# Handing the last three token tiles to the first expert by one-hot products, with its first weights split during the attention

## The chip, the cores and the metric

The kernel runs on one core of a Trainium2 chip (trn2). The metric is the device time of one execution in microseconds (us), as the median of several runs. One execution is also recorded by the hardware profiler; its rows are the trace. In the rows, PE is TensorE (matmuls), PEld its weight loads, DVE is VectorE, ACT is ScalarE, POOL is GpSimd and SP is SyncE, which issues most of the DMA transfers; PEclk is the clock granted to TensorE as a share of 2.4 GHz, so that 0.50 is 1.2 GHz. Times in the trace count from the start of the recorded span.

## What is computed

Three stages follow one another. The attention takes 2 batches of 8 heads, 768 tokens of 64 numbers each, and masks every pair of tokens whose clusters differ. Its result is read as 1536 tokens of 512 numbers. A mixture of 8 experts then sends each token through the one expert that it picks (512 to 1024, ReLU, and back to 512). A bilinear layer ends the kernel. Everything is float32.

```python
scores = scale * np.matmul(q, k.transpose(0, 1, 3, 2))
scores = np.where(mask, scores, -1000000000.0)
attn = np.exp(scores - max); attn = attn / (sum + 1e-09)
x = (attn @ v).transpose(0, 2, 1, 3).reshape(B * S, H * D)
# experts
expert_idx = np.argmax(xn @ en.T / tau, axis=1)
for e in range(E):
    mask = expert_idx == e
    h = np.maximum(x[mask] @ w1[e], 0.0)
    out[mask] = gate_w[mask, None] * (h @ w2[e])
# bilinear
return (out @ w_a) * (out @ w_b) @ w_out
```

## The kernel before

**Order.** The kernel is written under a manual schedule: each engine runs its instructions in the order in which the Python code issues them, and an engine stands at an instruction until the semaphores that it waits for have come. The issue order is the only plan there is.

**Attention.** There are 96 steps, twelve for each of eight pairs (batch, two heads). Step s issues: the exponentials E(s+1) (ACT, L478), the six transposes et(s) (PE, L493) and their two copies to SBUF, ET (half on ACT at L497, half on DVE at L499), the scores sc(s+2) (PE, L464 and L465), their row maximum nmx(s+2) (DVE, L473), and then pieces of older work from Python generators: the products pv with the values (PE, L520), their copy xt (ACT, L526), the product px that turns the result back into token rows and gives the expert logits (PE, L534), and the scaled rows xrow and xlog (DVE, L536). Steps 84 to 95 are the last pair. Token rows come in tiles of 128; a batch has six, 0 to 5, and those of the second batch are finished in groups: tiles 0 to 2, then 3 and 4, then 5. So et_90 below means the transposes of step 90, and px_7_5 the product px of pair 7 for tile 5.

**Picking and routing.** For each group, `pick_gen` finds every token's expert (the one-hot array oh_all), and `route_gen` counts, with small matmuls pos on PE, which slot of its expert the token gets; slot_i holds the slots. An expert has CAP = 256 slots. POOL then writes the rows of each tile to their slots in the DRAM tensor xs_d, one indirect DMA for a tile (the scatter, L584). After the last group, cnt_p (L717) counts the tokens of each expert, and `most` (L721) is the fullest expert's count. Every engine loads `most` into a register (L906) and branches on it (L907): code for experts with over 256 tokens is skipped here.

**Experts.** The weights of an expert come as chunks of 512x512, in parts of 128x512, which SP loads into `raw` (L129). Each part is split into a high part w hi (ACT cast, L818) and a low part w lo (DVE subtraction, L824), and a product is the sum of three matmuls (high by high, high by low, low by high). Before the branch ACT casts the eight parts of the first two chunks, `split_hi(8)`; after the branch DVE subtracts them, `split_lo()`. Beside that SP loads the 256 rows of expert 0 from xs_d (`load_xe(0)`, behind all scatters), PE keeps busy with 14 matmuls on dummy data (`keep_warm`, wps) and transposes the rows (`trans_x`, xT, L888), and ACT and DVE split them (xTh, L890, and xTl, L892). The main loop then counts G from 0 to 63 for eight experts of eight blocks: `layer1(G)` issues h (twelve matmuls, L900), ACT's ReLU hh (L967) and DVE's rest hl (L968); `layer2(G-2)` issues y (six matmuls, L983).

**Gates.** In the later experts the generator `gates()` advances once for each G. After some arithmetic it issues, for each of the twelve token tiles, one POOL scatter of 8-byte rows into the DRAM table tab_d (L782), each followed by a POOL memset of one element of `tick` (L787).

Of the kernel before, what the change touches and what calls it, by code (L numbers as in the profile page):

```python
# [22 lines left out]
P = 128  # L23
FAR = float(2.0 ** 100)
CAP = 256
# [10 lines left out]
FL3 = 14  # L36
# [6 lines left out]
def kernel(  # L43
# [39 lines left out]
    psa = att_stack.enter_context(tc.tile_pool(name="psa", bufs=1, space=PSUM))  # L83
# [33 lines left out]
    def load_raw():  # L117
# [12 lines left out]
        for j in range(cnt):  # L130
            raw[m + j] = t[:, j]

# [371 lines left out]
    def pv_gen(g, between=None):  # L504
# [10 lines left out]
        per, every = ((3 if t0 else 2), 1) if pp == NP - 1 else (2, 2)  # L515
# [17 lines left out]
        for t in range(n):  # L533
            nc.tensor.matmul(px[:, t, :], xt[:, t * P:(t + 1) * P], rmat[:, hp, :], start=True, stop=True)  # L534
        for c0, w, dst in ((2 * D, NE, lg[:, tsl, 2 * hp * NE:2 * (hp + 1) * NE]), (0, D, xs[:, tsl, 2 * hp * D:2 * (hp + 1) * D])):
# [30 lines left out]
    def route_gen(b, t0, n):  # L566
# [7 lines left out]
        for j in range(n - 1):  # L574
            nc.tensor.matmul(pp_[:, j + 1:, :], ones, oh[:, j:j + 1, :].to_broadcast([P, n - 1 - j, NE]), start=False, stop=(j == n - 2))
        sl = rt.tile([P, HALF, NE], F32, tag="r_sl", name=f"sl_{b}_{t0}", bufs=2)[:, :n]
        nc.vector.tensor_tensor(out=sl, in0=pp_, in1=oh, op=ALU.mult)
        with nc.allow_low_precision(reason="one whole number below 2^24 and zeros"):
            nc.vector.tensor_reduce(out=slot_i[:, gsl], in_=sl, axis=AX.X, op=ALU.add)
# [10 lines left out]
        for j in range(n):  # L590
            yield
            junk = rt.tile([P, DM], F32, tag="r_junk", name=f"junk_{b}_{t0}_{j}")
            nc.scalar.activation(junk, x_rows[b][:, t0 + j, :], AF.Square, accum_out=n2_all[:, gsl.start + j:gsl.start + j + 1])
# [57 lines left out]
    for s in range(nst):  # L651
# [14 lines left out]
        if s in (4 * SPP + 1, 4 * SPP + 3, 4 * SPP + 7, 4 * SPP + 9):  # L666
            load_raw()
        if s + 1 < nst:
            expo(s + 1)
        etrans(s)  # L670
        if 2 <= s < SPP:
            next(rest, None)
# [19 lines left out]
        if s + 1 == nst or steps[s + 1][0] != g_:  # L692
            def then(g=g_):
# [4 lines left out]
                elif s + 1 < nst:  # L698
# [4 lines left out]
                    yield from route_gen(b, t0, n)  # L703
                else:
                    yield from pv_gen(g, pick_gen(b, t0, n))
# [5 lines left out]
    work = later + work  # L711
    while work:
        work = [g for g in work if next(g, 0) != 0]


    cnt_p = psa.tile([P, NE], F32, tag="rot", name="cnt_p", bufs=3)
    nc.tensor.matmul(cnt_p, ones, cum.rearrange("p o e -> p (o e)"), start=True, stop=True)  # L717
    cnt = left.tile([P, NE, 1], F32, name="cnt")
# [47 lines left out]
    def gates():  # L766
# [14 lines left out]
        for g in range(B * NT):  # L781
# [5 lines left out]
            nc.gpsimd.memset(tick[:, g:g + 1], 0.0)  # L787
# [7 lines left out]
    ps_s = ctx.enter_context(tc.tile_pool(name="ps_s", bufs=2 * CT, space=PSUM))  # L795
    ps_t = ctx.enter_context(tc.tile_pool(name="ps_t", bufs=1, space=PSUM))
    big = ctx.enter_context(tc.tile_pool(name="big", bufs=1))

# [4 lines left out]

    def open_part():
        n, j = divmod(nsplit[0], 4)
        if j == 0:
            hl[n] = big.tile([P, 2, 4, 512], F32R, tag=f"w{n % NSLOT}", name=f"w_{n}")
        w = raw.pop(nsplit[0])
        nsplit[0] += 1
        return w, hl[n][:, 0, j, :], hl[n][:, 1, j, :]  # L810

    halves = []

    def split_hi(m):
        for _ in range(m):
            load_raw()
            w, hi, lo = open_part()
            nc.scalar.copy(hi, w)  # L818
            halves.append((w, hi, lo))

    def split_lo():
        while halves:
            w, hi, lo = halves.pop(0)
            nc.vector.tensor_sub(lo, w, hi)  # L824
            ndone[0] += 1
            load_raw()

    def split_some(m):
# [321 lines left out]
```

## Time and profile before

| what | value |
|---|---|
| time of the kernel before, median of 3 runs | 821.48 us (821.29 to 823.35) |
| time of the profiled execution | 823.11 us |
| span of its trace | 821.4 us |
| PE busy | 787.9 us, 96% of the span |
| DVE busy | 487.4 us, 59% |
| ACT busy | 397.9 us, 48% |
| POOL busy | 90.8 us, 11% |

PE is busy nearly all the time, so what can be won lies where it is not. The page cuts the span into 40 slices; PE falls below nine tenths in the first slice and in slices 15 and 16 (the way from the attention to the experts, about 288 to 308 us), and in slice 22 (435 to 442 us, amid the experts), and its clock falls with it. How to read a row of a timeline: start, length, engine, line, operation, what it writes <- what it reads, shape, count, and in brackets how long the engine stood idle before it and whose end let it go.

### The profile page before, as it was taken

To read this page: it belongs to the slowest core of one execution; us is meant where nothing else is said; L and a number is where in the kernel's file an instruction comes from. 1 tells how busy PE (TensorE), PEld (TensorE's weight loads), DVE (VectorE), ACT (ScalarE), POOL (GpSimd) and SP (SyncE) were. 2 spreads that over 40 slices of the span, in tenths; PEclk is the share of its full clock that TensorE was granted. 3 is DMA by queue.
4 is the path that set the end of the run, shared out by engine and by line. 5 is a ranking of instruction groups with operands and counts; after the bars stand their busy time and mean duration, and the time that the engine had idled before them with its cause. 6 is when DMAs were issued, how large, how long until landed. Compare 5 with 4: busy or idle time off the path is not lost.

```text
span 821.4 us, 13806 instructions
## 1 busy us (share of the span) xinstructions
PE 787.9 (96%) x5359; PEld 675.5 (82%) x5359; DVE 487.4 (59%) x996; ACT 397.9 (48%) x859; POOL 90.8 (11%) x122
## 2 busy tenths in 40 slices
PE   8899999999999949999997999999999999999997
PEld 5667777776777629999996999999999999999996
DVE  7777577775767557886674699999432222222221
ACT  4666766766666546765553555555221221211211
POOL 5212203233000030000023000000010010010101
PEclk9999999999999979999998999999999999999999
DMA  6137313353120038987768766764010000000000
GB/s 194 41 100 251 85 31 97 74 169 93 30 59 10 1 121 306 322 283 232 226 189 176 220 215 188 241 201 139 1 53 27 26 26 1 1 26 1 28 1 26
DMA packets 45388, 92.62 MB, mean 113 GB/s; under 512 B 6265, under 2 KB 15097, under 8 KB 45313
## 3 DMA queue, kind: packets, MB, share of 16 engines
q1 hardware_dynamic: 41104, 81.67, 33.5%
q0 software_dynamic: 2304, 6.31, 2.0%
q10 hardware_dynamic: 1904, 3.67, 1.3%
q8 instruction: 44, 0.72, 0.4%
q14 instruction: 32, 0.25, 0.1%
HBM read 69.27 MB, written 14.69 MB: 102 GB/s over the span
## 4 chain that ended last, share of the span: by engine, by line
PE 33%; issue 26%; another core or an unknown queue 1%; POOL 1%; DVE 1%; ACT 0%; POOLq 0%; DVEq 0%; ACTq 0%
PE h L900 11%; PE y L983 10%; PE ab L900 8%; PE o L1053 3%; POOL out_dram L1064 1%; PE xT L888 1%; DVE w L824 1%; ACT w L818 0%; POOLq L1145 0%; POOL tick L1069 0%; ACT hh L967 0%; DVE ot L1063 0%; DVE xTh L890 0%; PE xT_('b', 0)_0_6645 L888 0%
## 5 line engine op out<-in xcount | busy, mean ns | idle before, releaser
L1026 DVE TENSOR_TENSOR ga<-ab,ga 128x256 f32<-128x256 f32 x72 | 30.5, 423 | 153.5 <-ACT ga L1025 153.5
L478 ACT ACTIVATE E<-sc,nmx 128x768 f32<-128x768 f32 x96 | 86.7, 903 | 58.7 <-DVE nmx L473 46.1
L1025 ACT COPY ga<-ab 128x256 f32<-128x256 f32 x72 | 26.8, 372 | 164.6 <-PE ab L900 164.6
L473 DVE TENSOR_REDUCE nmx<-sc 128x1 f32<-128x768 f32 x96 | 91.4, 953 | 16.8 <-PE sc L465 15.1
L493 PEld LDWEIGHTS et<-ident,E 128*128 128x128 f32 x576 | 62.5, 141 | 36.1 <-ACT ET L497 12.6
L1053 PE MATMUL o<-w,gh 128*128 128x512 f32 x288 | 90.7, 396 | 0.0
L824 DVE TENSOR_TENSOR w<-raw,w 128x512 fp32r<-128x512 f32 x128 | 82.5, 687 | 13.4 <-ACT w L818 12.0
L493 PE MATMUL et<-ident,E 128*128 128x128 f32 x576 | 82.3, 279 | 5.8 <-ACT E L478 4.3
L499 DVE COPY ET<-et 128x384 f32<-128x384 f32 x96 | 52.7, 549 | 55.0 <-PE et L493 52.2
L983 PE MATMUL y<-w,hh 128*128 128x512 f32 x256 | 81.6, 400 | 0.5 <-issue 0.5
L900 PEld LDWEIGHTS h<-xTh,w 128*128 128x128 f32 x512 | 71.2, 194 | 13.2 <-DVE hl L968 4.8
L818 ACT CAST w<-raw 128x512 fp32r<-128x512 f32 x128 | 72.9, 619 | 18.4 <-DMA raw<-in_moe_w_dram 12.1
L900 PE MATMUL h<-xTh,w 128*128 128x256 f32 x512 | 73.5, 287 | 7.4 <-DVE hl L968 4.4
L520 PE MATMUL pv<-ET,v 128*64 128x384 f32 (+2 forms) x408 | 73.2, 479 | 0.8 <-ACT ET L497 0.6
L464 PE MATMUL sc<-K,Q 80*128 80x512 f32 x192 | 72.7, 379 | 0.0
L465 PE MATMUL sc<-K,Q 128*128 128x512 f32 x192 | 61.3, 340 | 0.0
L967 ACT ACTIVATE hh<-h 128x256 fp32r<-128x256 f32 x64 | 24.5, 383 | 66.8 <-PE h L900 56.6
L1053 PE MATMUL o<-w,gl 128*128 128x512 f32 x144 | 56.1, 389 | 0.0
L1029 ACT CAST gh<-ga 128x256 fp32r<-128x256 f32 x72 | 29.3, 407 | 53.6 <-DVE ga L1026 53.6
L1053 PEld LDWEIGHTS o<-w,gh 128*128 128x128 f32 x288 | 49.6, 190 | 6.5
L1064 POOL DMA_INDIRECT out_dram<-ot,res x12 | 11.5, 958 | 364.9 <-DVE ot L1063 363.6
L983 PE MATMUL y<-w,hl 128*128 128x512 f32 x128 | 50.0, 391 | 0.0
(266 smaller groups left out, 1498.3 us busy)
## 6 DMA issues: line engine op xcount, KB each, us to landing
raw<-in_moe_w_dram SPq DMA_DIRECT2D x64, 512.0 KB
raw<-in_moe_w_a_dram SPq DMA_DIRECT2D x12, 512.0 KB
raw<-in_moe_w_b_dram SPq DMA_DIRECT2D x12, 512.0 KB
raw<-in_moe_w_out_dram SPq DMA_DIRECT2D x12, 512.0 KB
xs_d<-zero SPq DMA_DIRECT2D x8, 512.0 KB
ys_d<-ys SPq DMA_DIRECT2D x8, 512.0 KB
xe<-xs_d ACTq DMA_DIRECT2D x7, 512.0 KB
v<-in_v_dram SPq DMA_DIRECT2D x8, 384.0 KB
```

The lines of the kernel that those rows point to most:

```text
L464: nc.tensor.matmul(ps[:, lo:hi], Q3[:, qs], K3[:, h * S + lo:h * S + hi], start=True, stop=False)
L465: nc.tensor.matmul(ps[:, lo:hi], Q2[:, qs], K2[:, h * S + lo:h * S + hi], start=False, stop=True)
L473: nc.vector.tensor_reduce(out=nmx[pp][:, h, t:t + 1], in_=sc[s], axis=AX.X, op=ALU.max, negate=True)
L478: nc.scalar.activation(e, sc.pop(s), AF.Exp, bias=nmx[pp][:, h, t:t + 1], accum_out=sums[pp][:, t, h:h + 1])
L493: nc.tensor.transpose(pt[:, j * P:(j + 1) * P], e[:, kt * P:(kt + 1) * P], ident)
L499: nc.vector.tensor_copy(dst, src)
L520: nc.tensor.matmul(pv[h * D:(h + 1) * D, :], vt[:, h, kt, :], ets[g, h][:, kt, :n * P], start=(kt == 0), stop=(kt == NT - 1))
L818: nc.scalar.copy(hi, w)
L824: nc.vector.tensor_sub(lo, w, hi)
L900: nc.tensor.matmul(ps, s_, m_, start=(i == 0), stop=(i == len(ops) - 1))
L983: nc.tensor.matmul(ys_ps[e][t], s_[:, t * P:(t + 1) * P], w[:, m_, ff, :], start=(f == 0 and i == 0), stop=(f == NF - 1 and i == 2))
L1053: nc.tensor.matmul(o_ps[ck][t], s_[:, t * P:(t + 1) * P], w_[:, m_], start=(f == 0 and i == 0), stop=(f == NF2 - 1 and j == len(o_f[ck]) - ...
```

## The change

There are five edits, all in one kernel file.

1. **One-hot products.** The rows of the last three token tiles of the second batch (3, 4 and 5) no longer reach expert 0 through DRAM. Once the nine other tiles are scattered, SP loads expert 0's rows (`near_load`). PE transposes them with eight plain matmuls against the identity into two PSUM tiles (`near_trans`), and for each of the three tiles eight more matmuls (`inject`) add the tile's rows, as high and low parts, times a one-hot matrix of slots. The scatters of these three tiles still go out, for the experts behind. The one-hot matrices come from ACT (Abs, then Relu) for tiles 3 and 4 and from DVE for tile 5. The high and low parts of the rows are made during the attention for the columns of the first six heads (a cast of 128x1152 on ACT, a subtraction on POOL), and at the end for the rest.
2. **The end of the attention.** The product pv_7_0 runs in two pieces of six instead of three of four, tiles 0 to 2 are picked and routed some steps earlier, the squares of the rows (junk) are reordered, and the last work list is walked in reverse.
3. **First weights.** The four parts of the first chunk, w_0, are split in steps 85 to 88 (`split_some(1)`), the next two before the branch (`split_hi(2)`). `keep_warm(14)`, `load_xe(0)` and `trans_x` of expert 0 are gone; `load_xe(1)` is issued in block G = 1.
4. **Branch.** The condition has a label and a hint for PE that the branch is likely taken, and the new pools wait for single tiles instead of for the whole pool before them.
5. **Gates.** The memset of `tick` after each scatter into tab_d becomes a copy of one element of the newest hh.

```diff
-    def pv_gen(g, between=None):
+    def pv_gen(g, between=None, behind_px=None):
-        per, every = ((3 if t0 else 2), 1) if pp == NP - 1 else (2, 2)
+        per, every = (3, 1) if pp == NP - 1 else (2, 2)
...
+        if near and t0 > HALF:
+            inject(1)
...
+                nc.scalar.activation(far, near_t["iota"], AF.Abs, bias=ns[:, j:j + 1])
+                nc.scalar.activation(near_t["oneh"][:, j, :], far, AF.Relu, scale=-1.0, bias=1.0)
...
+    def near_hi(t0, n, c0, c1):
+        nc.scalar.copy(near_t["hi"][:, t0:t0 + n, c0:c1], x_rows[B - 1][:, HALF + t0:HALF + t0 + n, c0:c1])
+    def near_load():
+        i = nc.sync.dma_start(out=near_t["xe"], in_=xs_d[:CAP, :].rearrange("(c p) d -> p c d", p=P))
+    def near_trans():
+        near_t["ps"] = [psa.tile([P, 2, CAP], F32, tag="sc", name=f"xT_near_{u}", bufs=2) for u in range(2)]
+        for j in range(DC):
+            for t in range(CT):
+                nc.tensor.matmul(near_t["ps"][j // 2][:, j % 2, t * P:(t + 1) * P], near_t["xe"][:, t, j * P:(j + 1) * P], ident,
+                                 start=(j % 2 == 0 and t == 0), stop=False)
+    def inject(t):
+        for j in range(DC):
+            for k_ in ("hi", "lo"):
+                nc.tensor.matmul(near_t["ps"][j // 2][:, j % 2, :], near_t[k_][:, t, j * P:(j + 1) * P], near_t["oneh"][:, t, :],
+                                 start=False, stop=(t == HALF - 1 and j % 2 == 1 and k_ == "lo"))
...
+        if s == (NP - 1) * SPP + SPP // 2 + 1:
+            near_hi(0, HALF, 0, 2 * (HP - 1) * D)
+            near_lo(nc.gpsimd, 0, HALF, 0, 2 * (HP - 1) * D)
+        if s == (NP - 1) * SPP + 10:
+            near_load()
         if s + 1 < nst:
             expo(s + 1)
         etrans(s)
+        if pp == NP - 1 and i in (1, 2, 3, 4):
+            split_some(1)
...
+    tc.mark_branch_hint_location("rare", "LikelyTaken", engines=[mybir.EngineType.PE])
...
-            nc.gpsimd.memset(tick[:, g:g + 1], 0.0)
+            nc.gpsimd.tensor_copy(tick[:, g:g + 1], hh()[0:1, 0:1])
...
-    load_xe(0)
-    split_hi(8)
+    split_hi(2)
     n_most = nc.values_load(most, min_val=0, max_val=NTOK)
-    with tc.If(n_most > CAP):
+    with tc.If(n_most > CAP, label="rare"):
...
-    keep_warm(ps_s.tile([P, DM], F32, tag="sc", name="wps2"), FL3)
     split_lo()
-    trans_x(0, xe_t[0], True)
-    load_xe(1)
...
+            if G == 1:
+                load_xe(1)
```

The first place is DVE in steps 85 and 86. A row gives the line, the operation, what it writes <- what it reads, and the semaphores waited for. Before:

```order
L473 TENSOR_REDUCE nmx_2979<-sc_3028 128x1 [waits PE_49]
L499 COPY ET_0_0_3017<-et_1_3045 128x3x128 [waits PE_49]
L473 TENSOR_REDUCE nmx_2979<-sc_3050 128x1 [waits PE_49]
L499 COPY ET_0_0_3017<-et_1_3063 128x3x128 [waits PE_49]
L473 TENSOR_REDUCE nmx_2979<-sc_3068 128x1 [waits PE_49]
```

and in the changed kernel:

```order
L505 TENSOR_REDUCE nmx_2980<-sc_3035 128x1 [waits PE_49]
L531 COPY ET_0_0_3024<-et_1_3052 128x3x128 [waits PE_49]
L156 TENSOR_TENSOR w_3057<-raw_1929,w_3057 128x512 [waits DMAHW2_49,Activation_49]
L505 TENSOR_REDUCE nmx_2980<-sc_3060 128x1 [waits PE_49]
L531 COPY ET_0_0_3024<-et_1_3073 128x3x128 [waits PE_49]
L156 TENSOR_TENSOR w_3057<-raw_1929,w_3057 128x512 [waits Activation_49]
L505 TENSOR_REDUCE nmx_2980<-sc_3082 128x1 [waits PE_49]
```

The subtraction w lo (L156) now stands between ET(s) and nmx(s+2), and it waits for ACT. On ACT the same steps of the changed kernel read:

```order
L510 ACTIVATE E_3045,sums_2979<-sc_3035,nmx_2980 128x768 [waits DVE_49,Activation_49]
L529 COPY ET_0_0_3024<-et_0_3047 128x3x128 [waits PE_49]
L150 CAST w_3057<-raw_1929 128x512
L510 ACTIVATE E_3066,sums_2979<-sc_3060,nmx_2980 128x768 [waits DVE_49,Activation_49]
L529 COPY ET_0_0_3024<-et_0_3068 128x3x128 [waits PE_49]
```

The cast w hi (L150) stands behind E(s+1) and ET(s) and ahead of E(s+2); before, E(s+2) followed ET(s) at once.

The second place is PE between the last px and the branch. Before, pos of tile 5 followed pos of tiles 3 and 4, and cnt_p and the load of `most` came right behind:

```order
L534 MATMUL px_5_3346<-rmat,xt_5_3342 128x144 [waits DVE_49,Activation_49]
...
L572 MATMUL pos_3_3351<-cum,ones 128x16 [waits PE_49]
...
L572 MATMUL pos_5_3374<-cum,ones 128x8 [waits PE_49]
L573 LDWEIGHTS tri
L573 MATMUL pos_5_3374<-oh_all,tri 128x8 [waits DVE_49]
L717 LDWEIGHTS ones [waits DVE_49]
L717 MATMUL cnt_p<-cum,ones 128x8 [waits PE_49]
L906 TENSOR_LOAD most [waits DVE_49]
L907 COMPARE_AND_BRANCH
```

In the changed kernel:

```order
L566 MATMUL px_5_3396<-rmat,xt_5_3374 128x144 [waits Activation_49]
L681 MATMUL xT_near_3398<-ident,xe_near 128x128 [waits DMAHW3_49]
L681 MATMUL xT_near_3398<-ident,xe_near 128x128 x3
L681 MATMUL xT_near_3399<-ident,xe_near 128x128 x4
L687 MATMUL xT_near_3398<-oneh,x_near_hi 128x256 [waits Activation_49]
L687 MATMUL xT_near_3398<-oneh,x_near_lo 128x256 [waits Pool_49]
...
L606 MATMUL pos_5_3426<-cum,ones 128x8 [waits PE_49]
L607 LDWEIGHTS tri
L607 MATMUL pos_5_3426<-oh_all,tri 128x8 [waits DVE_49]
L687 MATMUL xT_near_3398<-oneh,x_near_hi 128x256 [waits Activation_49]
```

Eight transposes, which wait for the load of xe_near, and the eight products of tile 3 now stand ahead of pos of tile 5; the products of tiles 4 and 5 follow around cnt_p.

The third place is POOL in the gates. Before:

```order
L782 DMA tab_d<-id_gate,slot_i 1536x2 [waits DMASW4_49,DVE_49,Pool_49]
L787 MEMSET tick 1x1
L782 DMA tab_d<-id_gate,slot_i 1536x2 [waits DMASW5_49]
L787 MEMSET tick 1x1
L782 DMA tab_d<-id_gate,slot_i 1536x2 [waits DMASW6_49]
```

In the changed kernel:

```order
L907 DMA tab_d<-id_gate,slot_i 1536x2 [waits DMASW4_49,DVE_49,Pool_49]
L913 CAST tick<-hh_5917 1x1 [waits Activation_49]
L907 DMA tab_d<-id_gate,slot_i 1536x2 [waits DMASW5_49]
L913 CAST tick<-hh_5948 1x1 [waits Activation_49]
L907 DMA tab_d<-id_gate,slot_i 1536x2 [waits DMASW6_49]
```

Between two scatters POOL now waits for the ReLU of one more block.

## Rows read from the trace of the kernel before

**Rows 1.** Windows: length, busy us of PE, PEld, DVE, ACT, POOL, clock, DMA, GB/s.
```profile
256.00:268.00 12.00, 12.00 (x80) 8.27 (x78) 8.11 (x13) 7.53 (x17) 0.00 (x0) 1.00 0.01 1
291.00:298.00 7.00, 0.48 (x4) 0.20 (x5) 2.72 (x19) 1.52 (x5) 4.42 (x11) 0.50 0.51 192
308.00:313.00 5.00, 5.00 (x29) 4.88 (x29) 1.99 (x4) 1.81 (x4) 0.00 (x0) 0.66 1.02 381
```
**Rows 2.** The page's groups of w lo and w hi: busy, mean ns, idle before.
```profile
L824 DVE TENSOR_TENSOR w<-raw,w 128x512 fp32r<-128x512 f32 x128 | 82.5, 687 | 13.4 <-ACT w L818 12.0
L818 ACT CAST w<-raw 128x512 fp32r<-128x512 f32 x128 | 72.9, 619 | 18.4 <-DMA raw<-in_moe_w_dram 12.1
```
**Rows 3.** Timeline of ACT in steps 85 to 89: start, length, operation.
```profile
258.48 0.90 ACT L478 ACTIVATE E<-sc,nmx 128x768 f32<-128x768 f32 x1 [0.24 <-DVE nmx L473]
...
259.37 0.47 ACT L497 COPY ET<-et 128x384 f32<-128x384 f32 x1
...
267.65 0.91 ACT L478 ACTIVATE E<-sc,nmx 128x768 f32<-128x768 f32 x1
```
**Rows 4.** Timeline of DVE in the same steps.
```profile
260.15 0.96 DVE L473 TENSOR_REDUCE nmx<-sc 128x1 f32<-128x768 f32 x1 [0.16 <-PE sc L465]
...
268.97 0.55 DVE L536 TENSOR_TENSOR xrow<-px,rs 128x384 f32<-128x384 f32 x1
```
**Rows 5.** Timeline of PE: the transposes of steps 90 and 95.
```profile
271.11 0.88 PE L493 MATMUL et<-ident,E 128*128 128x128 f32 x6
...
285.58 0.87 PE L493 MATMUL et<-ident,E 128*128 128x128 f32 x6
```
**Rows 6.** Timeline of PE from the last px to the first y.
```profile
289.00 0.51 PE L534 MATMUL px<-rmat,xt 128*128 128x144 f32 x2 [0.36 <-ACT xt L526]
...
302.57 1.04 PE L888 MATMUL xT<-ident,xe 128*128 128x128 f32 x8
304.06 0.74 PE L900 MATMUL h<-xTh,w 128*128 128x256 f32 x4 [0.46 <-ACT xTh L890]
307.35 0.74 PE L900 MATMUL h<-xTh,w 128*128 128x256 f32 x4 [2.55 <-DVE xTh L890]
...
313.02 0.63 PE L983 MATMUL y<-w,hh 128*128 128x512 f32 x2
```
**Rows 7.** Timeline of SP: the load of expert 0's rows.
```profile
298.78 0.37 SPq L875 DMA_DIRECT2D xe<-xs_d  x1
```
**Rows 8.** Timeline of POOL behind the last scatter.
```profile
295.96 0.20 POOL L728 MEMSET scan<- 128x24 f32 x2
```
**Rows 9.** Timeline of DVE: the end of the scan.
```profile
297.55 0.15 DVE L739 CAST ov_i<-cnt 1x8 int32<-1x8 f32 x1
```
**Rows 10.** The branch's line: sequencer, count, duration ns, first and last start.
```profile
L907 DVEq EVENT_SEMAPHORE  x2: 21/21/21, 300.9 to 301.0; - x2
...
L907 PEldq COMPARE_BRANCH  x1: 4112/4112/4112, 293.6 to 293.6; - x1
```
**Rows 11.** Windows amid the experts, same columns.
```profile
428.00:436.00 8.00, 8.00 (x54) 7.32 (x53) 4.05 (x7) 3.11 (x7) 6.68 (x13) 1.00 0.82 146
436.00:442.00 6.00, 1.61 (x7) 0.83 (x5) 0.01 (x1) 0.42 (x2) 3.23 (x8) 0.93 1.02 144
442.00:448.00 6.00, 5.53 (x23) 5.33 (x24) 4.33 (x9) 3.96 (x9) 0.00 (x0) 0.50 0.55 72
```
**Rows 12.** Timeline of POOL: the first and the last of twelve scatters into tab_d.
```profile
424.23 1.27 POOL L782 DMA_INDIRECT tab_d<-id_gate,slot_i  x1 [127.97 <-DVE w L824]
...
438.85 0.96 POOL L782 DMA_INDIRECT tab_d<-id_gate,slot_i  x1 [0.22 <-issue]
```
**Rows 13.** Timeline of ACT there: the ReLU that came last.
```profile
441.58 0.38 ACT L967 ACTIVATE hh<-h 128x256 fp32r<-128x256 f32 x1 [7.20 <-remote]
```
**Rows 14.** Timeline of PE there: the end of one h, the next that waited.
```profile
432.59 0.64 PE L900 MATMUL h<-xTl,w 128*128 128x256 f32 x4
...
442.47 2.08 PE L900 MATMUL h<-xTh,w 128*128 128x256 f32 x8 [4.37 <-DVE hl L968]
```

More of the change, by code (lines that the diff above doesn't have):

```diff
@@ L35 @@
 SP1 = 1
-FL3 = 14
 FL4 = 30
@@ L131, in load_raw, with open_part, split_hi, split_lo @@
             raw[m + j] = t[:, j]
+    def open_part():
+        n, j = divmod(nsplit[0], 4)
+        if j == 0:
+            hl[n] = (big if n % NSLOT else left).tile([P, 2, 4, 512], F32R, tag=f"w{n % NSLOT}", name=f"w_{n}")
+        w = raw.pop(nsplit[0])
+        nsplit[0] += 1
+        return w, hl[n][:, 0, j, :], hl[n][:, 1, j, :]
+    halves = []
+    def split_hi(m):
+        for _ in range(m):
+            load_raw()
+            w, hi, lo = open_part()
+            nc.scalar.copy(hi, w)
+            halves.append((w, hi, lo))
+    def split_lo():
+        while halves:
+            w, hi, lo = halves.pop(0)
+            nc.vector.tensor_sub(lo, w, hi)
+            ndone[0] += 1
+            load_raw()
+    def split_some(m):
+        for _ in range(m):
+            split_hi(1)
+            split_lo()
     qk_raw = {}
@@ L575, in route_gen @@
             nc.tensor.matmul(pp_[:, j + 1:, :], ones, oh[:, j:j + 1, :].to_broadcast([P, n - 1 - j, NE]), start=False, stop=(j == n - 2))
+        near = b == B - 1 and t0 >= HALF
+        if near and t0 > HALF:
+            inject(1)
         sl = rt.tile([P, HALF, NE], F32, tag="r_sl", name=f"sl_{b}_{t0}", bufs=2)[:, :n]
         nc.vector.tensor_tensor(out=sl, in0=pp_, in1=oh, op=ALU.mult)
[L578 to L579 removed]
+        if near and t0 > HALF:
+            ns = slot_n[:, t0 - HALF:t0 - HALF + n]
+            nc.vector.tensor_reduce(out=ns, in_=sl, axis=AX.X, op=ALU.add)
+            nc.vector.tensor_scalar(out=near_t["oneh"][:, t0 - HALF, :], in0=near_t["iota"], scalar1=ns, scalar2=None, op0=ALU.is_equal)
+            nc.vector.tensor_copy(slot_i[:, gsl], ns)
+        elif near:
+            ns = slot_n[:, :n]
+            nc.vector.tensor_reduce(out=ns, in_=sl, axis=AX.X, op=ALU.add, negate=True)
+            nc.vector.tensor_scalar(out=slot_i[:, gsl], in0=ns, scalar1=-1.0, scalar2=None, op0=ALU.mult)
+            for j in range(n):
+                far = rt.tile([P, CAP], F32, tag="r_far", name=f"far_{j}")
+                nc.scalar.activation(far, near_t["iota"], AF.Abs, bias=ns[:, j:j + 1])
+                nc.scalar.activation(near_t["oneh"][:, j, :], far, AF.Relu, scale=-1.0, bias=1.0)
+        else:
+            with nc.allow_low_precision(reason="one whole number below 2^24 and zeros"):
+                nc.vector.tensor_reduce(out=slot_i[:, gsl], in_=sl, axis=AX.X, op=ALU.add)
         for j in range(n):
@@ L710 @@
         work = [g for g, r in came if r is None]
-    work = later + work
+    work = (later + work)[::-1]
+    tc.mark_branch_hint_location("rare", "LikelyTaken", engines=[mybir.EngineType.PE])
     while work:
         work = [g for g in work if next(g, 0) != 0]
+    near_lo(nc.vector, HALF - 1, 1, 2 * (HP - 1) * D, DM)
     cnt_p = psa.tile([P, NE], F32, tag="rot", name="cnt_p", bufs=3)
     nc.tensor.matmul(cnt_p, ones, cum.rearrange("p o e -> p (o e)"), start=True, stop=True)
+    inject(HALF - 1)
+    for t in range(NT - HALF + 1, NT):
+        norms(B - 1, t)
     cnt = left.tile([P, NE, 1], F32, name="cnt")
@@ L802 @@
     lows = []
[L804 to L828, printed above, removed]
-        for _ in range(m):
-            split_hi(1)
-            split_lo()
     def narrow_a(m):
@@ L889, in trans_x @@
         for u in range(2):
-            (nc.vector.tensor_copy if u and first else nc.scalar.copy)(hi[:, 2 * u:2 * u + 2, :], pts[u])
+            nc.scalar.copy(hi[:, 2 * u:2 * u + 2, :], pts[u])
         for u in range(2):
```

70 lines of the change are left out of this document (56 added, 14 removed).

## The prediction, made before the changed kernel was run

> **What bounds the kernel now.** I read the page's slices first, then tables of windows around the slices in which PE is not full, then the timelines of each engine there. In the attention PE is full: 12.00 us busy of 12 at full clock between 256 and 268 us [rows 1]. Whatever makes PE wait there lengthens the kernel by as much. Two stretches leave PE empty. From 291 to 298 it works 0.48 us of 7 and its clock is at 0.50 (1.2 GHz); the first products behind, 308 to 313, still see 0.66 [rows 1]. Here everything waits for the last tiles to be routed, scattered and read back. The second stretch is amid the experts: from 436 to 442 PE works 1.61 us of 6, and from 442 to 448 it works 5.53 us, but at 1.2 GHz [rows 11]. In work at full clock that is 1.61 x 0.93 + 5.53 x 0.50 = 4.3 us of 12: the stall costs 7.7 us. It looks like this: h of a block ends at 432.59 + 0.64 = 433.23 [rows 14], but its ReLU hh starts only at 441.58, let go by something that the profile calls remote [rows 13], and the next h waits for hl until 442.47 [rows 14]. In that time POOL sends twelve scatters of 8-byte rows, from 424.23 to 438.85, (438.85 - 424.23) / 11 = 1.33 us apart [rows 12]. DMA is at 0.82, then at 1.02 of its time while it moves only 146 and 144 GB/s [rows 11]; in the weight-bound stretch 308 to 313 the same share moved 381 GB/s [rows 1]. I read this as a backlog of tiny writes that holds up the signals between engines.
>
> **The w_0 split in steps 85 to 88: +5.5 us.** Before, E(s+2) waited only for nmx(s+2), and PE, full, set the pace. Now ACT must do E(s+1), ET(s), w hi, and DVE then w lo ahead of nmx(s+2), which E(s+2) needs: a closed ring. One turn costs 259.37 - 258.48 = 0.89 for E and 0.47 for ET [rows 3], 0.62 for w hi and 0.69 for w lo [rows 2], and 0.96 for nmx [rows 4]: 3.63 us. Four turns put E_90 at 258.48 + 14.52 = 273.0, against 267.65 before [rows 3]: +5.35. PE had some room here, so not all of it arrives. nmx_90 ends just before E_90, at 272.9; behind it DVE does ET (about 0.5, as xrow), xlog (0.15, as the small operation in [rows 9]) and xrow (0.55) [rows 4], so xrow ends at 274.1 instead of 269.52 [rows 4], and et_90, which followed 1.59 us behind [rows 4, 5], moves from 271.11 to 275.7: +4.6. In steps 90 to 95, before 14.47 us long [rows 5], ACT gets a cast of 1152 columns (1152 / 512 x 0.62 = at most 1.4 us) and DVE the earlier picks and routes. I add 0.9, between 0 and 2 because these engines have idle time there. et_95 thus starts at 285.58 + 5.5 = 291.1 (290.1 to 292.2). POOL's subtraction of 1152 columns and its iota lie beside this, with nothing of POOL's due before the last tiles.
>
> **From et_95 to the first y: -5.4 us.** px_7_5 came 3.42 us behind et_95 [rows 5, 6]; two squares now stand ahead of its copy xt on ACT, at most 1.2 us by w hi. I take 4.0, so 295.1. On PE pos of tile 5 now stands behind near_trans and inject(0). A transpose takes 1.04 / 8 = 0.13 us [rows 6]; as plain float32 matmuls, which run as two records as px does [rows 6], eight cost 1.8 to 2.1. The eight products of inject cost 1.0 to 1.5 (0.74 for four h [rows 6], start included). xe_near must have landed: its load needs the scatters of tiles 0 to 2, whose routing is now some steps earlier; the old load took at most 302.57 - 298.78 = 3.8 us to the transposes that wait for it [rows 6, 7]. I place it about at px, so it costs 0 to 1. Then px 0.5, near_trans 1.8, inject 1.0: pos at 298.4. Four small operations of DVE follow (0.15 to 0.2 each, one of them the one-hot compare, 0.3), so the last scatter starts at 299.4. It takes 1.33 us of POOL by its pitch, so the memset of scan, before at 295.96 [rows 8], comes at 300.7: the wait for five scatters in a row is gone, but the routing ends later. From that memset the scan ended 297.70 - 295.96 = 1.74 us later [rows 8, 9], and DVE came back from the branch at 300.9, another 3.2 us later [rows 9, 10]. With two xTl subtractions ahead of the branch (0.69 each, partly hidden behind the scan's waits; I take 0.6) DVE is back at 306.2, and h_0, which in the changed program waits for a count that DVE gives behind the branch, starts at 306.5. PE's own branch (4.11 us [rows 10]), reached at about the time of that memset, would return by 305.5 without the hint, ahead of DVE: the hint saves nothing that counts.
>
> Before, h went on at 307.35, with four matmuls (0.5 us) done already [rows 6], and the first y came 5.67 us later, at 313.02 [rows 6]. So y_0 comes at 306.5 + 0.5 + 5.67 = 312.7. Without `keep_warm` PE idles some 6 us ahead of h. The old stretch lost 5 x (1 - 0.66) = 1.7 us to the clock [rows 1], so the work itself is 4.0 us; if the clock stays at half for all of it, 2.3 us are added, and if it is full, 1.7 saved. I take +0.4: y_0 at 313.1, so the way from the attention's start to y changes by +0.1. The bounds of the terms give -2.5 to +3. The later raw loads have two units more in hand, and load_xe(1) has a whole expert's time: nothing.
>
> **Pacing the scatters: -7.2 us.** POOL now waits for a new hh between scatters. A block has twelve h and six y matmuls, and 54 records took 8.00 us [rows 11]: 2.7 us a block, so the scatters spread over 32 us instead of 14.6. The stall ended at 441.58 [rows 13], 17.4 us behind the first scatter: an estimate of the drain is 17.4 / 12 = 1.45 us for each, well below 2.7, so no backlog grows. That a few scatters hurt nobody is seen from 428 to 436, when PE was full although POOL had begun at 424.23 [rows 11, 12]. The new wait behind it: an hh four blocks later needs the tick copy, 0.96 us [rows 12] behind hh, against 10.7 us of time. I leave 0.5 of the 7.7 for what single scatters still cost. The bounds are 0 and 7.7.
>
> **The sum.** The profiled execution took 823.11 us, 1.6 above the median of 821.48. 823.11 + 0.1 - 7.2 = 816.0 for such an execution; against the median, 821.48 + 0.1 - 7.2 = 814.4. I forecast 814.5.
>
> **Rivals.** *The stall stays.* If each scatter costs PE time by itself (7.7 / 12 = 0.64 us) and not by crowding, pacing only spreads the cost, and the kernel takes 821.5 + 0.1 = 821.6: no change. For it speaks that the DMA share was at its limit at 144 GB/s [rows 11], which is work and not waiting; against it the full PE from 428 to 436. [...]
>
> *The split is hidden.* If the ring is not closed as I read it, because ACT and DVE have idle time there (12 - 7.53 = 4.5 and 12 - 8.11 = 3.9 us of 12 [rows 1]), the attention ends 5.5 us sooner: 809.0. Against it: idle time does not help in a ring, where each waits for the other.
>
> *The clock falls in the attention* (the slower side). PE now idles about 40% of steps 86 to 89 (2.2 of 3.63 us busy). If the chip then grants 1.2 GHz, the 14.47 us of PE work from et_90 to et_95 [rows 5] take up to twice as long until the clock returns; at two thirds of that, +9.6: 824.1. It decides from the point where PE, at 60% busy, counts as idle. Rows show half clock only where PE was almost empty (0.48 of 7 [rows 1]; 1.61 of 6 ahead of the fall at 442 [rows 11]), so I hold it unlikely.
>
> **How the numbers follow.** Forecast 0.64 (its own range 811.5 to 818, from the terms' bounds), stall stays 0.14 (821.6), split hidden 0.13 (809.0), clock falls 0.09 (824.1). About 0.3%, 2.5 us, is what a measurement of this kernel can tell from no change. Faster by more than that: 0.64 + 0.13 = 0.77; within: 0.14; slower: 0.09. The range leaves out the slower rival and the lower half of the hidden one: 808.5 to 822.3.
>
> **What would show it.** Right: E spaced 3.6 us in steps 86 to 90; et_95 near 291; the memset of scan near 301; the first y within 2 us of 313; scatters into tab_d 2.7 us apart with PE full beside them. Wrong: E less than 3 us apart there (split hidden); a granted clock below 1 before 285 us; hh late by several us between 420 and 460 (stall stays); xe_near's transposes waiting for their load well past px.

## The result and the profile after

The changed kernel takes 813.61 us (813.36 to 815.21, 4 runs), the kernel before beside it 822.17 (821.29 to 823.35, 4 runs): the ratio is 0.990 (95% interval 0.988 to 0.992). The forecast was 814.5, in a range of 808.5 to 822.3. Of the two profiled executions one has a span of 821.4 us, the other of 812.0.

Where the 9.4 us between the two spans lie follows from the starts of five marks in both traces: the transposes of step 84, those of step 95, the first y, the first ab, and the last o.

| stretch | before, us | after, us | difference |
|---|---|---|---|
| start to et_84 | 255.62 | 256.20 | +0.6 |
| et_84 to et_95 | 29.96 | 35.88 | +5.9 |
| et_95 to the first y | 27.44 | 20.76 | -6.7 |
| first y to the first ab | 188.26 | 180.98 | -7.3 |
| first ab to the last o | 313.61 | 311.69 | -1.9 |

The 0.6 us at the start is probably not of the change. In this execution of the changed kernel the granted clock was 0.83 on average between 20 and 30 us (1.00 in that of the kernel before), and in another one on another chip, where it was 1.00 there, the changed kernel reached et_84 at 255.26:

```profile
20.00:30.00 10.00, 8.22 (x55) 6.37 (x54) 7.19 (x11) 5.83 (x13) 0.00 (x0) 0.83 0.05 19
```

(Length, busy us of PE, PEld, DVE, ACT and POOL, granted clock, DMA share, GB/s.) Now the attention. The timeline of ACT in the changed kernel (start, length, operation) answers to [rows 3]:

```profile
259.06 0.90 ACT L510 ACTIVATE E<-sc,nmx 128x768 f32<-128x768 f32 x1 [0.24 <-DVE nmx L505]
...
260.31 0.63 ACT L150 CAST w<-raw 128x512 fp32r<-128x512 f32 x1
262.62 0.90 ACT L510 ACTIVATE E<-sc,nmx 128x768 f32<-128x768 f32 x1 [1.69 <-DVE nmx L505]
...
273.32 0.90 ACT L510 ACTIVATE E<-sc,nmx 128x768 f32<-128x768 f32 x1 [1.31 <-DVE nmx L505]
```

The cast is done at 260.94, yet ACT stands idle for 1.69 us until nmx comes, which stands behind w lo on DVE:

```profile
260.97 0.69 DVE L156 TENSOR_TENSOR w<-raw,w 128x512 fp32r<-128x512 f32 x1 [0.39 <-ACT w L150]
261.58 0.95 DVE L505 TENSOR_REDUCE nmx<-sc 128x1 f32<-128x768 f32 x1
```

E follows E after 262.62 - 259.06 = 3.56 us; from E_86 to E_90 it is 14.26 us, against 9.17 before [rows 3].

The timeline of PE from just ahead of the transposes of step 90 to the first y answers to [rows 5, 6]:

```profile
274.42 2.47 PE L552 MATMUL pv<-ET,v 128*64 128x384 f32 x12 [0.65 <-DVE xrow L570]
276.82 0.87 PE L525 MATMUL et<-ident,E 128*128 128x128 f32 x6
...
292.08 0.88 PE L525 MATMUL et<-ident,E 128*128 128x128 f32 x6
...
296.03 0.51 PE L566 MATMUL px<-rmat,xt 128*128 128x144 f32 x2 [0.47 <-ACT xt L558]
296.39 2.05 PE L681 MATMUL xT_near<-ident,xe_near 128*128 128x128 f32 x16
...
299.27 0.17 PE L607 MATMUL pos<-oh_all,tri 128*128 128x8 bf16 x1
...
307.16 2.05 PE L1002 MATMUL h<-xTh,w 128*128 128x256 f32 x8 [5.44 <-DVEq L1007]
...
312.84 0.63 PE L1080 MATMUL y<-w,hh 128*128 128x512 f32 x2
```

The new transposes follow px at once, so the load of xe_near is no wait. The last line but one is the reading that counts: PE stands idle for 5.44 us until DVE's sequencer has come back from the branch at L1007. The routing ends on POOL (answers to [rows 8]) and the branch shows in its line (answers to [rows 10]):

```profile
300.66 0.96 POOL L636 DMA_INDIRECT xs_d<-xrow,slot_i  x1 [1.21 <-DVE x_near_lo L669]
...
301.64 0.20 POOL L853 MEMSET scan<- 128x24 f32 x2
```

```profile
L1007 DVEq EVENT_SEMAPHORE  x2: 21/21/21, 307.0 to 307.1; - x2
...
L1007 PEldq COMPARE_BRANCH  x1: 412/412/412, 301.7 to 301.7; - x1
...
L1007 DVEq COMPARE_BRANCH  x1: 72/72/72, 303.9 to 303.9; - x1
```

PE's branch takes 0.41 us with the hint, not 4.11, and PE still waits until 307.1 for DVE, which needs 3.1 us from its own branch to its next instruction. Without dummies PE's granted clock falls meanwhile, to 0.50 from 304 to 310. The windows (length, busy us of PE, PEld, DVE, ACT and POOL, granted clock, DMA share, GB/s) in the attention (answers to [rows 1]), of this stretch, and amid the experts (answers to [rows 11]):

```profile
256.00:268.00 12.00, 9.86 (x66) 7.03 (x65) 7.48 (x13) 6.93 (x15) 0.00 (x0) 1.00 0.11 37
...
304.00:310.00 6.00, 2.84 (x13) 2.87 (x14) 1.86 (x3) 0.00 (x0) 0.00 (x0) 0.50 0.17 12
310.00:316.00 6.00, 6.00 (x45) 5.69 (x44) 5.40 (x11) 5.08 (x11) 0.00 (x0) 0.98 0.71 222
...
428.00:436.00 8.00, 8.00 (x53) 7.27 (x52) 5.71 (x10) 4.77 (x10) 3.47 (x6) 1.00 0.86 147
436.00:442.00 6.00, 6.00 (x42) 5.48 (x41) 3.71 (x7) 3.91 (x8) 2.32 (x4) 1.00 1.13 265
442.00:448.00 6.00, 6.00 (x41) 5.48 (x41) 4.36 (x8) 2.83 (x6) 2.32 (x4) 1.00 0.89 224
```

Amid the experts PE is now full at full clock where it had 1.61 us of 6. POOL's timeline shows the pace, one scatter for a block:

```profile
426.12 1.47 POOL L907 DMA_INDIRECT tab_d<-id_gate,slot_i  x1 [0.16 <-issue]
428.38 0.18 POOL L913 COPY tick<-hh 1x1 f32<-1x1 f32 x1 [0.80 <-ACT hh L1064]
428.72 0.98 POOL L907 DMA_INDIRECT tab_d<-id_gate,slot_i  x1 [0.16 <-issue]
```

### The profile page after: what moved, and what is told of

It is laid out like the page before. It is cut to its first block, busy times and chain, and to the rows that moved or that the text cites. A ratio compares the mean times of both kernels' runs of the same rounds, so it can differ in the third digit from the quotient of the medians.

```text
span 812.0 us, 13846 instructions
## 1 busy us (share of the span) xinstructions
PE 783.9 (97%) x5377; PEld 674.0 (83%) x5377; DVE 487.7 (60%) x1000; ACT 400.9 (49%) x867; POOL 95.2 (12%) x124
## 4 chain that ended last, share of the span: by engine, by line
issue 41%; PE 18%; DMA 2%; POOL 1%; POOLq 0%; ACT 0%; SPq 0%
PE h L1002 9%; PE y L1080 8%; DMA tab_d<-id_gate,slot_i 1%; POOL out_dram L1161 1%; PE xT L990 1%; DMA res<-tab_d 0%; POOLq L1244 0%; POOL tick L1166 0%; ACT w L150 0%; ACT hh L1064 0%; POOL tick L913 0%; POOLq L1161 0%; SPq L915 0%
## 5 line engine op out<-in xcount | busy, mean ns | idle before, releaser
L156 DVE TENSOR_TENSOR w<-raw,w 128x512 fp32r<-128x512 f32 x128 | 82.9, 688 | 17.1 <-ACT w L150 12.9
L150 ACT CAST w<-raw 128x512 fp32r<-128x512 f32 x128 | 73.3, 620 | 12.5 <-DMA raw<-in_moe_w_dram 12.4
```

## The experiments

Kernels of one group ran on one chip, beside runs of the kernel before on that chip. The chips differ: beside the first and second group the kernel before took 815.5 and 816.1 us, beside the third and the fourth 823.1 and 821.6, as at the time of the prediction (822.2). That turned out to be the key to the largest term. Each chip was used in one group only, so a difference between chips is not told apart here from one between the hours at which they ran.

### Group 1: the pace, the ring, the hint (kernel before: 815.48 us)

**Unpaced.** The changed kernel with the memset again.

```diff
-            nc.gpsimd.tensor_copy(tick[:, g:g + 1], hh()[0:1, 0:1])
+            nc.gpsimd.memset(tick[:, g:g + 1], 0.0)
```

> The changed kernel with one thing undone: behind each scatter into tab_d stands the memset of tick again, so the twelve scatters follow one another without waiting for a ReLU. If the pacing is what removed the stall (my theory), the stall comes back: scatters about 1.3 us apart, a ReLU late by some 8 us near 441 us, PE half idle from 436 to 442 at about the same place, and the time rises by 7.3 us (the way from the first y to the first ab was 188.3 us before and 181.0 in the changed kernel) to about 821. If the stall went for another reason (other times of the weight loads, other pools), PE stays full there and the time stays within 1 us of 813.6.

Measured: 813.76 us, and no stall. The scatters do follow one another closely, and PE is full beside them (POOL's timeline and the window):

```profile
437.11 0.95 POOL L907 DMA_INDIRECT tab_d<-id_gate,slot_i  x1 [0.22 <-issue]
...
438.68 0.96 POOL L907 DMA_INDIRECT tab_d<-id_gate,slot_i  x1 [0.54 <-DMA tab_d<-id_gate,slot_i]
```

```profile
436.00:442.00 6.00, 6.00 (x42) 5.48 (x41) 3.44 (x6) 2.87 (x6) 4.01 (x8) 1.00 1.05 217
```

My expectation missed. But the kernel before, too, was 6 to 7 us faster here than at first, so the stall might simply not exist on this chip, and the run could not decide.

**Paced.** The kernel before with the copy of hh in `gates()`, and nothing else.

```diff
-            nc.gpsimd.memset(tick[:, g:g + 1], 0.0)
+            nc.gpsimd.tensor_copy(tick[:, g:g + 1], hh()[0:1, 0:1])
```

> The kernel before with one part of the change: the memset of tick becomes the copy of one element of the newest hh. If pacing is worth its 7.3 us by itself and all other edits sum to nothing, this gives 821.5 - 7.3 = about 814, equal to the changed kernel within 1 us. If the rest of the change has a part in the gain, it lands between 815 and 821.

Measured: 816.40 us, ratio 1.0012 (1.0002 to 1.0021) to the kernel before: a miss again. Beside a kernel before that shows no stall by its times, the pace wins nothing, and costs at most 0.2%.

**The subtraction behind the row maximum.**

```diff
         if pp == NP - 1 and i in (1, 2, 3, 4):
-            split_some(1)
+            split_hi(1)
...
             scores(s + 2)
             rowmax(s + 2)
+        split_lo()
```

> The changed kernel with the four subtractions w lo of steps 85 to 88 moved behind the row maximum nmx of the step after next; the casts w hi stay. If the ring E, ET, w hi, w lo, nmx is what delays the attention, E follows E by 2 to 3 us again instead of 3.57, the transposes of step 95 start about 5 us earlier (287 instead of 292.1), and the time falls by 4 to 5.5 us to 808 to 809.5. If ACT's cast ahead of E or the sheer load of DVE is to blame, the spacing stays above 3 us and the time falls by less than 2 us.

Measured: 810.22 us, ratio to the kernel before 0.994 (0.992 to 0.996), 3.5 us below the unpaced kernel of the same group, which has the ring and is otherwise the changed kernel but for the pace (the next experiment has ring and pace, without the hint, and takes 814.12). The fall is a little less than forecast: 0.7 us remain above the range of 808 to 809.5. The timelines of ACT and of PE:

```profile
259.97 0.90 ACT L510 ACTIVATE E<-sc,nmx 128x768 f32<-128x768 f32 x1 [0.24 <-DVE nmx L505]
...
269.18 0.92 ACT L510 ACTIVATE E<-sc,nmx 128x768 f32<-128x768 f32 x1
```

```profile
288.54 0.87 PE L525 MATMUL et<-ident,E 128*128 128x128 f32 x6
```

From E_86 to E_90 it is 9.21 us, as before the change (9.17), though the same casts and the same subtractions are done there. The load of the two engines was not the cost, but the place of w lo in the ring. From et_84 to et_95 it is 31.4 us instead of 35.9; this attention began about 1 us later, so et_95 stands at 288.5. Over the 29.96 of before 1.5 us are left. Of these 0.7 lie ahead of et_90, where PE now runs twelve matmuls of pv in 2.16 us and before the change ran eight in 1.51 (the larger pieces of the second edit), and 0.8 in steps 90 to 95, as in the changed kernel; which of the work moved there costs them was not tried.

**No hint.**

```diff
-    tc.mark_branch_hint_location("rare", "LikelyTaken", engines=[mybir.EngineType.PE])
```

> The changed kernel without the branch hint for PE. If PE waits for DVE's return from the branch (my theory), PE's branch takes about 4.1 us again instead of 0.41 and returns near 305.8, still ahead of DVE at 307.1, and the time stays within 0.5 us. If PE's return is what starts the first h, the time rises by up to 3.7 us.

Measured: 814.12 us, against 813.76 for the unpaced kernel beside it, which has the hint. The branch and the first h:

```profile
L1006 PEldq COMPARE_BRANCH  x1: 3852/3852/3852, 302.6 to 302.6; - x1
```

```profile
307.88 2.05 PE L1001 MATMUL h<-xTh,w 128*128 128x256 f32 x8 [5.30 <-DVEq L1006]
```

PE's branch costs 3.85 us again, and the first h still waits for DVE: the hint alone bought nothing, as forecast.

### Group 2: both kernels again, and all repairs together (kernel before: 816.05 us)

**The kernel before, the changed and the unpaced kernel** once more, without an edit of their own.

> The kernel before once more, beside the changed one on the same chip, because the runs beside the first four experiments gave 815.5 us for it instead of 821 to 823. If the 7.7 us stall amid the experts belongs to the program, its trace shows PE half idle from 436 to 442 again and 821 us. If it belongs to the chip or the load of the day, the trace shows PE full there, y-to-ab takes about 181 us instead of 188.3, and the time is near 815.

> The changed kernel once more beside the kernel before. Where the kernel before shows its stall, it is 7 to 9 us faster; where the kernel before shows none, only the 1.9 us of the bilinear layer and the 0.2 us of the way to the first y are left: about 2 us faster (813.5).

> The changed kernel with the memset of tick, as in the first experiment. On a chip where the kernel before shows the stall: 821 if pacing removes it, 813.6 if another part of the change does. On a chip where it does not: 813.6, and nothing is told.

Measured: 815.88, 813.44 and 814.23 us. In the trace of the kernel before, PE is full in the window in which it had 1.61 us at first [rows 11], although POOL sends most of its scatters 1.26 us apart here too (1.40 on average, 1.33 at first):

```profile
436.00:442.00 6.00, 6.00 (x42) 5.48 (x42) 3.44 (x7) 2.87 (x6) 4.46 (x8) 1.00 1.08 203
```

From the first y to the first ab it takes 181.2 us, and the bilinear layer the same 313.6 as at first. So the stall does not belong to the program alone: the same program took 188.3 us in this stretch at first, and what differs is the chip, or the hour. Where it is missing, the change is worth only the rest: 813.44 against 816.05, ratio 0.9975 (0.9965 to 0.9984).

**All repairs.** The subtraction behind the row maximum, the hint for DVE too, and 13 dummy matmuls behind the last one-hot products.

```diff
-    tc.mark_branch_hint_location("rare", "LikelyTaken", engines=[mybir.EngineType.PE])
+    tc.mark_branch_hint_location("rare", "LikelyTaken", engines=[mybir.EngineType.PE, mybir.EngineType.DVE])
...
     inject(HALF - 1)
+    keep_warm(psa.tile([P, DM], F32, tag="rot", name="wps2", bufs=3), FL3)
```

> The changed kernel with the subtractions w lo behind the row maximum, with the branch hint given to DVE too, and with 13 dummy matmuls on PE behind the last one-hot products. Attention as in the third experiment: 4.4 us sooner. [...] Together 813.6 - 8.3 = 805.3; with neither of the two, 809.2.

Measured: 806.13 us, ratio to the kernel before 0.988 (0.987 to 0.990), 7.3 us below the changed kernel on the same chip. The branch's line, and the first h:

```profile
L1010 DVEq EVENT_SEMAPHORE  x2: 21/21/21, 299.3 to 299.4; - x2
...
L1010 PEldq COMPARE_BRANCH  x1: 3924/3924/3924, 296.4 to 296.4; - x1
...
L1010 DVEq COMPARE_BRANCH  x1: 90/90/90, 298.6 to 298.6; - x1
```

```profile
300.76 1.18 PE L1005 MATMUL h<-xTh,w 128*128 128x256 f32 x8 [1.54 <-PEq L1010]
```

DVE needs 0.7 us behind its branch, not 3.1, and eight h take 1.18 us, not 2.05: both repairs work. The 8.3 us of the expected sum are 4.4 for the attention and 3.9 for the way behind it; the 3.9 were my estimate of what DVE's return and the held clock would save together, and no run shows them. Of the 7.3 us measured the traces put 4.5 into the attention (from et_84 to et_95 31.4 us for 35.9) and 3.3 into the way from et_95 to the first y (18.3 for 21.7), and 0.6 are lost again behind it. But PE's own branch takes 3.92 us in spite of its hint, and now PE comes last, 1.1 us behind DVE.

### Group 3: dummies, and the stall at last (kernel before: 823.11 us)

**No dummies, six dummies.** The kernel of all repairs with none, and with 6 instead of 13.

```diff
-FL3 = 13
+FL3 = 6
```

> The eighth kernel without its 13 dummy matmuls: w lo behind the row maximum, and the branch hint for PE and DVE. There PE's branch took 3.92 us in spite of the hint, and PE came back 1.1 us behind DVE. If the 26 instructions added in front of the branch are what spoils PE's hint, PE's branch takes 0.41 us here as in the changed kernel, h starts with DVE's return, 1.1 us sooner than in the eighth kernel, but at 1.2 GHz for part of the first products: 805.5 to 807. If DVE's hint spoils PE's, PE's branch stays near 3.9 us and the time is 806.5 to 808.

> The eighth kernel with 6 dummies instead of 13. If any instruction added there spoils PE's hint, PE's branch stays at 3.9 us and the time at 806 to 807. If it is the place of the branch in the code, it may be 0.41 us here, and with the clock held the time is 804.5 to 805.5.

Measured: 809.27 us without (ratio 0.981, 0.979 to 0.984) and 807.07 with six (0.979, 0.977 to 0.981). Both lie above the ranges forecast for a branch of 0.41 us, by 2.3 and 1.6 us. In their traces 2.2 to 2.3 us more lie ahead of step 84, against the kernel with 13 dummies: the granted clock was 0.66 between 20 and 30 us here and 1.00 there. The four runs of each spread over 4 us, so these medians tell little of 1 or 2 us, and what follows is read from the stretches of the traces. PE's branch is at 0.41 us in both; the first line is of the kernel with six. Then the first h of each, first without, then with six dummies:

```profile
L1010 PEldq COMPARE_BRANCH  x1: 408/408/408, 298.7 to 298.7; - x1
```

```profile
302.14 2.04 PE L1003 MATMUL h<-xTh,w 128*128 128x256 f32 x8 [3.05 <-DVEq L1008]
```

```profile
301.83 1.18 PE L1005 MATMUL h<-xTh,w 128*128 128x256 f32 x8 [1.75 <-DVEq L1010]
```

So neither the dummies as such nor DVE's hint spoil PE's hint; 26 instructions more in front of the branch went with a slow one and 12 did not, in one trace each and on two chips. Why is open. The dummies are worth 3.1 us by themselves in this stretch: from et_95 to the first y it takes 20.2 us without and 17.1 with six, most of it because without them nearly all of the first h run at a granted clock of 0.50, which lasts from 302 to 308 in the kernel without; this window shows its beginning.

```profile
302.00:304.00 2.00, 1.86 (x9) 1.90 (x10) 1.29 (x2) 0.00 (x0) 0.00 (x0) 0.50 0.06 16
```

That is also why DVE's hint brings little alone: without dummies the first h starts 13.2 us behind et_95 instead of 15.1 in the changed kernel, but the first y comes only 0.5 us sooner (20.2 for 20.8).

In the kernel with six the next bound shows on ACT: the weights themselves come late, and 2.0 of the 3.1 us are lost again before the first ab.

```profile
311.60 1.14 ACT L151 CAST w<-raw 128x512 fp32r<-128x512 f32 x2 [3.00 <-DMA raw<-in_moe_w_dram]
```

**Unpaced, a third time.**

> The changed kernel with the memset of tick, a third time, in case this chip shows the stall of the first profile (then the kernel before takes 821 to 823 beside it). Where it does: 821 if the pacing is what removes the stall, 814 if it is another part of the change. Where the kernel before takes 814 to 816: 813.5 to 814.5, the same as the changed kernel, and the pacing is worth nothing there.

Measured: 821.45 us, ratio to the kernel before 0.998 (0.997 to 0.999), while the two paced kernels of this group, which have the repairs besides, take 807 and 809. The windows and ACT's timeline:

```profile
436.00:442.00 6.00, 3.46 (x21) 2.60 (x19) 0.00 (x0) 0.00 (x0) 4.73 (x10) 0.96 0.89 189
442.00:448.00 6.00, 3.65 (x17) 3.65 (x18) 3.52 (x7) 3.11 (x7) 0.00 (x0) 0.50 0.21 29
```

```profile
443.46 0.38 ACT L1064 ACTIVATE hh<-h 128x256 fp32r<-128x256 f32 x1 [8.64 <-remote]
```

This is the stall of [rows 11, 13], in a kernel that has every part of the change but the pace: PE half idle, then at a granted clock of 0.50, and a ReLU let go 8.64 us late. From the first y to the first ab it takes 188.3 us, as before the change; in the paced kernels on the same chip 181.2 (no dummies) and 183.2 (six; part of its excess is the late weights). So the other parts of the change do not remove the stall by themselves. No two runs on this chip differ in the pace alone; the changed kernel, which differs from this one in nothing else, had none in the first comparison (181.0 us), beside a kernel before that stalled.

### Group 4: an address (kernel before: 821.6 us)

**The low slot.** The kernel before, with one weight slot in the pool that is open from the start: in the compiled programs it holds every ninth chunk, 0, 9, 18, 27 and 36 (the expectation says every eighteenth).

```diff
-            hl[n] = big.tile([P, 2, 4, 512], F32R, tag=f"w{n % NSLOT}", name=f"w_{n}")
+            hl[n] = (big if n % NSLOT else left).tile([P, 2, 4, 512], F32R, tag=f"w{n % NSLOT}", name=f"w_{n}")
```

> The kernel before with one thing moved: the SBUF tile that holds every eighteenth weight chunk (chunks 0, 18 and 36) lies in the pool that is open from the start, at another address, as in the changed kernel; the order of work stays. If this address is what makes the ab matmuls with chunk 36 start every 113.4 ns instead of 119 to 120, the bilinear layer takes 311.7 us from the first ab to the last o instead of 313.6, and the time falls by 1.9 us against the kernel before beside it. If the new pools' waits or the other order do it, both stay as they were.

Measured: 819.0 us, ratio 0.998 (0.995 to 1.001): by time unclear. The stall hides an effect of this size: the runs spread from 816.8 to 826.9 us, and the trace shows a stall that is smaller than the first one. A ReLU is let go 6.78 us late, PE is busy for 3.51 us of 6 and keeps its clock, and from the first y to the first ab it takes 185.2 us, between the 181 and the 188 seen so far.

```profile
438.89 0.38 ACT L967 ACTIVATE hh<-h 128x256 fp32r<-128x256 f32 x1 [6.78 <-remote]
```

```profile
436.00:442.00 6.00, 3.51 (x22) 2.72 (x21) 1.72 (x3) 1.54 (x4) 3.49 (x8) 1.00 0.96 196
```

The bilinear layer, behind the stall, tells more. Eight ab matmuls with chunk 36 in the kernel before, in the changed one, and in this one:

```profile
550.45 1.12 PE L900 MATMUL ab<-xTh_('b', 0)_6643,w 128*128 128x256 f32 x8
```

```profile
542.75 1.07 PE L1002 MATMUL ab<-xTh_('b', 0)_6674,w 128*128 128x256 f32 x8
```

```profile
545.90 1.11 PE L900 MATMUL ab<-xTh_('b', 0)_6643,w 128*128 128x256 f32 x8
```

From start to start they take 120, 113.4 and 117.8 ns; with the other chunks it is 119 to 120 in all three kernels. In the compiled programs the chunk lies at byte 44,320, 18,688 and 19,552 of a partition. First ab to last o takes 313.6, 311.7 and 313.0 us. Chunk 36 is read by 288 of the 1,728 ab matmuls, and 288 x 6.6 ns is the 1.9 us, 288 x 2.2 ns the 0.6 us. So moving the slot (other tiles of its new pool shift with it, the other weight chunks stay where they were) does change the pace of these matmuls here, from 120 to 117.8 ns, but it brings only a third of the 6.6 ns; what it is in the move that counts is open, and that the other two thirds come from the slot's place too is not shown.

## Why the prediction was right, and where

**The split in the attention (+5.5 forecast, +5.9 measured).** The ring turned as worked out: 3.56 us for 3.63, and E_90 came 14.26 us behind E_86 for 14.52. et_90 moved by 5.1 us against et_84, for 4.6, and steps 90 to 95 by 0.8, for 0.9. The ring was thus 0.3 us cheaper than worked out, and the place of et_90 behind it 0.8 us later. I had let et_90 follow xrow as before, and left out the larger pieces of pv: PE runs twelve matmuls there in 2.47 us, where it ran eight in 1.51 before:

```profile
269.67 1.51 PE L520 MATMUL pv<-ET,v 128*64 128x384 f32 x8
```

The third experiment shows that the place of w lo makes 4.5 of the 5.9 us.

**From et_95 to the first y (-5.4 forecast, -6.7 measured).** Term by term, behind et_95: px at 3.95 us (4.0), pos at 7.2 (7.3), the last scatter at 8.6 (8.3), the memset of scan at 9.56 (9.6), h at 15.1 (15.4). The last scatter came 0.3 us late, but only 0.98 us ahead of the memset, not 1.33. The term that was mis-sized is the last: the first y came 5.68 us behind the first h, not 6.57. I had charged 0.5 for the four h done early and 0.4 for the clock. Neither shows: 36 h took the time of 32 before. The clock was back sooner (0.50 until 310.2 and full behind, 3.0 us behind the first h, where it had been 0.50 from 308.0 to 311.4), and the four h with xTl, which before took 1.19 us from their start to the next, took 0.86. That the hint would save nothing, since DVE comes last, held.

**The pace (-7.2 forecast, -7.3 measured).** At the time of the prediction and on the chip of the third group the step held: with the scatters spread, the late ReLUs are gone, and from the first y to the first ab it takes 181.0 us for 188.3 in the first comparison and 181.2 and 183.2 for 188.3 in the third group, whose paced kernels have the repairs besides. That a backlog of writes holds up signals is still my reading of the rows. The profile names no releaser for those ReLUs, only `remote`, and no run tests it; the DMA share, which I took as a sign, is 1.08 and 1.13 between 436 and 442 in traces without a stall. What I did not see is that the stall need not come with the program. The four groups ran on four chips, and on two of them the kernel before took 815.5 and 816.1 us; the traces taken there show scatters nearly as close (1.38 to 1.40 us apart on average, 1.31 and 1.33 in the traces with the full stall) and no stall. There the whole term is missing, and the gain falls to 2.6 us. That the term which I forecast from one trace was there in the result is the luck of the chip. One reading was wrong without effect: the 0.96 us of [rows 12] is the length of a scatter, and the copy of tick takes 0.18. As far as these runs go, the stall came only in kernels whose scatters stand in a row (1.31 and 1.33 us apart in the two traces with the full stall), but not in all of their runs. What a chip or the hour adds to it stays open.

The rival *the stall stays* fails on the chip that stalls: the cost does not stick to each scatter, since the paced kernels send the same twelve and take 181.0 to 183.2 us from the first y to the first ab, not 188.3. And where there is no stall, PE is full even beside scatters in a row: 6.00 us of 6 between 436 and 442 in the unpaced kernel of the first group and in the kernel before of the second.

The rival *the split is hidden* fell with the spacing of E, 3.56 us. The rival of the falling clock fell by its price, not by its premise. In the first trace the granted clock stayed at 1.00 from 256 to 298, though PE had only 9.86 us of 12 between 256 and 268. But of the five later traces with the ring (unpaced three times, no hint, the changed kernel again) four show it at 0.50 for 3.4 us between 266 and 272, which I had named as a sign of being wrong. Here the changed kernel again:

```profile
267.20:270.40 3.20, 3.20 (x12) 1.49 (x11) 1.99 (x3) 1.58 (x4) 0.00 (x0) 0.50 0.06 23
```

It cost nothing: from et_84 to et_95 all six traces take 35.8 to 35.9 us. PE, which waits for the ring there, had the time to run slower.

**The bilinear layer (nothing forecast, -1.9 measured).** I looked only at what the change reorders, and not at what it moves in memory. Between the two profiled executions the sum is -9.4 for a forecast of -7.1: this gain and the 1.3 us more on the way to y, the pace's 0.1, less 1.0 us more that the start and the attention lose. The medians moved by 8.6 us. That the time came out so near, 813.6 for 814.5, is also the work of the median from which I set out, 821.48 of three runs; with the fourth it is 822.17.

## What to carry to other kernels

Work put into idle time of two engines is free only if it does not lie between a result and the engine that waits for it: look at the order on each engine, close the ring, and add it up; here four subtractions one place further back were worth 3.5 us. A hint for one engine pays nothing while another comes last: PE's alone was worth nothing (813.76 us with it, 814.12 without). DVE's, without dummies, brought the first h 1.9 us sooner and the first y 0.5; with dummies that hold the clock as well, the first y came 2.4 to 3.7 us sooner behind the attention (18.3 and 17.1 us for 20.8). Many small scatters in a row should be paced by the work beside them (from the first y to the first ab 181.0 us for 188.3 where the stall showed; where none did, a cost of at most 0.2%), and a stall that is won or lost should be looked for on more than one chip before it is booked. A fallen clock should be priced by who waits for the slowed engine: at 0.50 between 266 and 272 PE cost the attention nothing (35.8 to 35.9 us with the fall and without), and at 0.50 on the first products eight h took 2.04 us for 1.18.

## What the runs showed of the hardware that was not expected

The kernel before took 815.5 and 816.1 us beside the first two groups and 823.1 and 821.6 beside the other two, each on a chip of its own, and the traces put this into one stall beside twelve scatters of 8-byte rows. From the first y to the first ab it takes 188.3 us in two traces with the stall (the kernel before at first, the unpaced kernel of the third group), 185.2 in a third (the low slot), and 181.2 in the trace of the kernel before that has none. What brings the stall on is open.

A branch hint that runs at the start of the program, at 0.9 us in the trace of the changed kernel and some 1,960 matmul records ahead of the branch on PE, still went with a branch of 0.41 us on PE, for 3.85 without it in the same group; a hint for DVE went with 0.7 us behind DVE's branch, for 3.1. Without the hint PE's branch took 4.11 us in two traces of the kernel before and 3.85 in the changed kernel; with it and 13 dummy matmuls in front 3.92, with six dummies 0.41. What fills the time where it is long is not shown.

Eight ab matmuls with chunk 36 started every 120 ns in the kernel before, every 117.8 in the one with the moved slot and every 113.4 in the changed kernel, at a granted clock of 1.00 and with PE full. The three programs have this chunk at different places of a partition; whether it is the place that makes the difference is shown only as far as the moved slot goes, 2.2 of the 6.6 ns.
